# Two more Strassen-like inner products in a layernorm-MLP kernel on Trainium2

## The chip, the cores and the metric

The kernel runs on one core of a Trainium2 chip. The metric is the device time of one execution in microseconds (us), lower is better. Times come from a profiled execution (the profile) and from unprofiled repeats; the median of the runs is what is compared.

## The reference

The kernel computes a layernorm over the last axis, a first matrix product with gelu, and a second matrix product, for 2048 rows, D = 1024 and F = 3584, with bf16 inputs and outputs:

```
def reference(x, w1, b1, w2, b2):
    y = _layernorm(x, axis=-1)
    h = _gelu(jnp.einsum("bsd,df->bsf", y, w1) + b1)
    return jnp.einsum("bsf,fd->bsd", h, w2) + b2
```

## The kernel before

The 2048 rows are worked off in two blocks of 1024 (block 0 and block 1). Each block has a first stage, MM1 (y times w1, with gelu on ScalarE, called ACT), and a second stage, MM2 (h times w2 plus b2). Both use a fast matrix multiplication in place of the plain one: the 2x2 block product is formed from seven products instead of eight, with sums of operand quarters ("S" sums of the left operand, "T" sums of the right one) and sums of the products. The sums run on VectorE (DVE), the matmuls on TensorE (PE).

In MM2 a product, numbered 1 to 7, multiplies a quarter of h, or a sum of quarters (S1 to S4, made in place in h by `sums`, hS1 to hS4), with a quarter of w2 (B11, B12, B21, B22) or a sum of quarters (T1 to T4). T1 to T4 of w2 are made once, in MM1 of block 0, by `w2_prep` (line 702), and stored to a DRAM buffer (`w2_sums`) from which later loads take them. T1 also stays in SBUF, in the slot A of `w2a_sb`; B11 lies in slot B.

A product of MM2 is done in one of two ways:

- plain (`plain`, line 793): four row tiles, 14 matmuls of 512 columns each, 56 in all;
- inner (`inner`, line 838): the same seven-product scheme once more, one level down. Its steps run in the order 1, 5, 6, 2, 7, 3, 4; each is 14 matmuls of 256 columns, 98 in all. It needs four S sums and four T sums of its own (128x1792 elements each, line 681), and copies or additions of PSUM between the steps: step 6 waits for a copy of step 1's result (f1, or s2/k1), step 7 for a copy or an addition of step 6's result (k2), step 4 for an addition after step 7 (r22 or o22). In the form without an output f1, k5, k2, r11 and r21 are ACT copies and r22, r12 DVE additions; in the form with an output k1 and the seed s2 are ACT copies.

Which products are inner is a table, and so is their order:

```
SEQ2 = ((5, 1, 2, 6, 7, 3, 4), (1, 5, 2, 6, 7, 3, 4))
INNER = ((1, 2, 3, 4), (1, 5, 2, 7, 3, 4))
```

So in block 0 products 5, 6 and 7 are plain, and in block 1 product 6 alone. The inner T sums of products 1 to 4 are formed in block 0 by `inner_sums` (line 814) and stored to DRAM (`w_inner_sums`); those of products 5 and 7 are formed in MM1 of block 1 by `t_inner` (line 1130), which loads T1 or T3 back from DRAM. Block 1 loads all of them with `fetch` (line 965), seven loads of 448 KB for a product.

Beside MM2 of block 0 run the x tiles of block 1: `ln_act2` (line 438) does the layernorm of eight tiles on ACT (a sum, a scale, the squares, and at the end the normalization, L459), with three small POOL steps (L450, L453, L456) between the squares and the normalization. Then SP, which issues the DMAs, issues two DMA transposes for each tile (`dma_T`, L488).

The order on every engine is fixed beforehand by a planner (`Planner.place`): each operation has an engine, a cost and a due time, and the planner places it in the engine's queue by these. Each engine then takes its instructions in this order, and waits on semaphores. The buffers that sums are written to are those of MM1 (`t1_sb`, and the three slots of `w1_sb`), as they come free.

Of the kernel before, what the change touches and what calls it, by code (L numbers as in the profile page):

```python
# [23 lines left out]
P = 128  # L24
# [7 lines left out]
SEQ2 = ((5, 1, 2, 6, 7, 3, 4), (1, 5, 2, 6, 7, 3, 4))  # L32
INNER = ((1, 2, 3, 4), (1, 5, 2, 7, 3, 4))
# [203 lines left out]
def bass_standalone__mixer_channel_mlp__prompt_kernel(  # L237
# [24 lines left out]
    with ExitStack() as es:  # L262
# [58 lines left out]
        T_MM2 = TH * 3 * NU * MM512 + 4 * 7 * NU * MM256  # L321
# [112 lines left out]
        junk2 = t1_sb[:, :, :, :, :].rearrange("p a b k c -> p (a b k c)")[:, 7 * D:8 * D]  # L434
# [3 lines left out]
        def ln_act2(s, i, prio, war):  # L438
            war = [*war, *junk_last[-1:]]
            a0 = add("ACT", 1.25, lambda e: e.activation(out=junk2, in_=x_sb[:, i, :], func=ACT.Identity,  # L440
# [4 lines left out]
            a2 = add("ACT", 1.35, lambda e: e.activation(out=junk2, in_=x_sb[:, i, :], func=ACT.Square,  # L445
# [292 lines left out]
        def load_w2(s, slot, what, deps, prio):  # L738
            if what in W2SRC:
                e, c = W2SRC[what]  # L740
                o = dma(w2q[slot], w2v[:, e, :, c * HT:(c + 1) * HT], deps, prio, f"w2_{s}_{what}", f"w2_{slot}",
                        NU * P * HT * 2)
                return w2q[slot], [[o]] * NU
            j = int(what[1]) - 1
            o = dma(w2q16[slot], tq[j], [*deps, *tq_ok[j]], prio, f"w2_{s}_{what}", f"w2_{slot}", NU * P * HT * 2)
            return w2q16[slot], [[o]] * NU
# [3 lines left out]
        def mm2_block(s, W):  # L750
# [3 lines left out]
            for p in SEQ2[s]:  # L754
                pt[p] = t0
                t0 += 7 * SUB if p in inn else TH * SLOT2
            A = {q: (h[q], [[h_ok[(s, q, u)]] for u in range(NU)]) for q in h}
            users = {p: [] for p in SEQ2[s]}
            stores = []
            done = lambda p: users[p]  # L760
# [22 lines left out]
            def dve(fn, deps, at, name, **k):  # L783
                return add("DVE", 0.69, fn, deps, at, name, **k)
# [52 lines left out]

            def inner(p, a, Yo, xb, war, O=None, bias=None, out=None, gate=(), kk=None):

# [60 lines left out]
                hk = Holder(snaps) if kk is None else None  # L900

                def kk_q():
                    t = kk if hk is None else sn_sb[:, hk.k, :]
                    return t.rearrange("p (v c) -> p v c", v=2)
# [5 lines left out]
                k1 = copy(kk_q, lambda: bank_q(c0), (subs[1], *gate), end(1), f"k1_{nm}", alloc=hk)  # L910
                k5 = dve(lambda e: plus(e, quart(g, 1, 1), bank_q(c5), quart(g, 1, 1)), (subs[5], ok[22]), end(5), f"k5_{nm}")
                sub(6, (k1,))
                k2 = dve(lambda e: plus(e, quart(g, 0, 1), bank_q(c0), quart(g, 0, 1)), (subs[6], ok[12]), end(6), f"k2_{nm}")
# [4 lines left out]
                o22 = dve(lambda e: plus(e, o_q(1, 1), bank_q(c0), quart(g, 1, 1)), (subs[7], k5), end(7), f"o22_{nm}",  # L918
                          alloc=ho[1])
                sub(3, (k5,))  # L920
                o12 = dve(lambda e: plus(e, o_q(0, 1), bank_q(c5), quart(g, 0, 1)), (subs[3], k2, o11), end(3), f"o12_{nm}",
                          frees=(c5,))
                if out is not None:
# [3 lines left out]
                          f"o21_{nm}", frees=(c0, g) if out is not None else (c0,))  # L927
                if out is not None:
                    store(out, 2, 2, ho[1], (o22, o21), end(4))
                users[p] += list(subs.values()) + flat(s1, s2, s3, s4)  # L930
                if out is None:
                    return g, {11: o11, 12: o12, 21: o21, 22: o22}, subs
# [6 lines left out]
            X0 = halves(t1_sb[:, :, :, :, :].rearrange("p a b k c -> p (a b k c)"))  # L939
            n = s * NC + NC - 1  # L940
            Y0 = [y for m in (n - 2, n) for y in halves(w1_16[:, m % N_W1].rearrange("p k c -> p (k c)"))[:2]]
            S1 = sums(h[21], A[21], A[22], ALU.add, (), pt[5] - 12, f"hS1_{s}")
            ring = uniq(*(w1_use[m] for m in range(n - 2, n + 1)), *(l for m in (n - 1, n) for l in t1_use[m].values()))
            war0 = {(c, r): ring + S1[1][-1] for c in "ST" for r in range(1, 8)}

            def last_block():
# [39 lines left out]
                def give(names, subs):  # L986
                    for r, b in zip(SEQ1, names):
# [3 lines left out]
                        2: ("W0", "W1", "Y5", "Y6", "Y7", "X0", "X1"), 7: ("B0", "B1", "B2", "B3", "V0", "V1", "Y0"),  # L991
                        3: ("Y1", "Y2", "Y3", "Y4", "W0", "W1", "Y5"), 4: ("Y6", "Y7", "X0", "X1", "A0", "A1", "A2")}
                Yo = {1: fetch(1, hold[1], base1[s] + 0.5 * T_MM1), 5: fetch(5, hold[5], pt[1] - 10),
                      2: fetch(2, hold[2], pt[1])}
                ring_of = lambda m: [*w1_use[m], *(o for l in t1_use[m].values() for o in l)]
                warX = {("S", r): ring_of(n - 1) + (ring_of(n) if r in (7, 3) else []) for r in (5, 6, 7, 3)}
# [10 lines left out]
                B6 = load_w2(s, "A", "T2", [o for k in range(4) for o in use[f"A{k}"]], pt[5])  # L1007
                Yo[7] = fetch(7, hold[7], pt[2])
                hb = [Holder(banks, seeded=True) for _ in range(TH)]
                sdb = seed(1, hb, lambda t: tile_of(g1, t), [(ok1[11], ok1[12]) if t < 2 else (ok1[21], ok1[22])  # L1010
                                                             for t in range(TH)], pt[2])
                S2 = sums(h[11], S1, A[11], ALU.subtract, done(1), pt[5] + 2, f"hS2_{s}", step=(2, 4, 4, 4))
                S3 = sums(h[21], A[22], S2, ALU.subtract, done(5), pt[2] + 4, f"hS3_{s}", step=(4, 4, 4, 2))

                okw = {11: ok1[11], 12: sdb[1], 21: sdb[3], 22: sdb[3]}
                sub2 = inner(2, A[12], Yo[2], XX, war_of(sub1), O=(g1, okw), out=11, gate=W["x"])
# [3 lines left out]

                M6 = plain(6, S2, B6, hb, False, [(o,) for o in sdb])
                g12, gv = Holder(snaps, 4), Holder(snaps, 4)
                O12, V = [], []
                for t in range(TH):
                    at = pt[6] + (t + 1) * SLOT2
                    ok_t = (ok5[11], ok5[12]) if t < 2 else (ok5[21], ok5[22])
                    V.append(copy(lambda t=t: tile_of(gv, t), lambda t=t: bank_t(hb[t]), (M6[t], *V[:1]), at, f"V_{s}_{t}",
                                  alloc=gv if t == 0 else None))
                    O12.append(dve(lambda e, t=t: plus(e, tile_of(g12, t), bank_t(hb[t]), tile_of(g5, t)),
                                   (M6[t], V[t], *ok_t, *O12[:1]), at, f"O12_{s}_{t}", alloc=g12 if t == 0 else None,  # L1030
                                   frees=(hb[t],)))
                for k in range(4):
                    use[f"A{k}"] = list(M6)
                Yo[4] = fetch(4, hold[4], pt[7])

                okv = {11: V[1], 12: V[1], 21: V[3], 22: V[3]}
                gw, okq, sub7 = inner(7, S3, Yo[7], XT, war_of(sub5), O=(gv, okv), kk=dl_sb[:, :], gate=(sub5[5],))
                give(hold[7], sub7)
                for i in range(2):
                    ho = Holder(outs, 2)  # L1040
                    f = []
                    for j in (1, 0):
                        q = 10 * (i + 1) + j + 1
                        f.append(dve(lambda e, i=i, j=j, ho=ho: plus(
                            e, o_sb[:, ho.k:ho.k + 2, j * HI:(j + 1) * HI], quart(gw, i, j), quart(g5, i, j)),
                            (okq[q], O12[3], *f), pt[7] + 7 * SUB + 0.1 * i, f"o22_{s}_{i}{j}",
                            alloc=ho if not f else None, frees=(g5,) if i and not j else ()))
                    store(22, 2 * i, 2, ho, f, pt[7] + 7 * SUB)

                sub3 = inner(3, S4, Yo[3], XX, war_of(sub2),  # L1050
                             O=(g12, {11: O12[1], 12: O12[1], 21: O12[3], 22: O12[3]}), out=12)
                inner(4, A[22], Yo[4], XT, war_of(sub7), O=(gw, okq), out=21,
                      gate=(f[-1],))
# [8 lines left out]
            B = dict(W)  # L1062

            h5 = [Holder(banks, seeded=True) for _ in range(TH)]
            sd5 = seed(5, h5, lambda t: dl_sb[:, :].rearrange("p (j c) -> p j c", j=2), [(bias_ok, jobs[-3])] * 2 + [(bias_ok, jobs[-1])] * 2, pt[5] - 8)
            M5 = plain(5, S1, B[5], h5, False, [(o,) for o in sd5])
            g5 = Holder(snaps, 4)
            O5 = []
            for t in range(TH):
                O5.append(copy(lambda t=t: tile_of(g5, t), lambda t=t: bank_t(h5[t]), (M5[t], *O5[:1]),  # L1070
                               pt[5] + (t + 1) * SLOT2, f"O5_{s}_{t}", alloc=g5 if t == 0 else None, frees=(h5[t],)))

            B[2] = load_w2(s, "C", "B21", W["C"], base2[s])
            B[6] = load_w2(s, "A", "T2", done(5) + tq_ok[0], pt[1])
            hb = [Holder(banks, seeded=True) for _ in range(TH)]
            g1, ok1, sub1 = inner(1, A[11], inner_sums(1, B[1], Y0, war0), X0, war0, gate=(M5[2],), bias=(
# [187 lines left out]
```

## Time and profile before

| | |
|---|---|
| median of 4 runs (range) | 344.26 us (343.61 to 345.03) |
| profiled execution, its time | 345.03 us |
| its span | 343.30 us |
| PE, DVE, ACT, POOL busy | 335.3, 259.3, 184.0, 23.5 us |
| MM1 of block 0 | up to 99.8 us |
| MM2 of block 0: product 5 | 99.80 to 111.88 us |
| MM2 of block 0: products 1, 2, 6, 7, 3, 4 | 111.88 to 184.03 us, overlapping MM1 of block 1 from 174.26 us |
| MM1 of block 1 | to 263.53 us |
| MM2 of block 1 | 263.53 to 339.82 us |

The stages are those of the chain of waits, in which TensorE's groups are merged in order of time. L608 are the matmuls of MM1, L797 those of plain and L864 those of inner products. Instructions of one line in a row are counted with "x", the time from a group's start to the next one's is what the group took on PE. Timelines give start, duration, engine, line, operation, output and inputs; what stands in brackets is the engine's idle time ahead of the instruction and what ended it.

### The profile page before, as it was taken

What the parts mean: (1) busy time and instruction counts of PE and PEld (TensorE: products, weight loads), DVE (VectorE), ACT (ScalarE), POOL (GpSimd) and SP (SyncE); (2) the same over time, 40 slices, a digit from 0 to 9 for tenths busy, and PEclk for the clock granted to TensorE, in tenths of its full rate; (3) what the DMA queues carried; (4) which work ended last, traced back from release to release, by engine and by line L of the source; (5) the groups of instructions that cost most, each with busy time, mean ns of one, the idle gap of its engine ahead of it and who ended that gap; (6) DMA issues with size and microseconds to landing.
All of it is one profiled execution on the core that took longest, in us unless ns stands there. A gap on an engine that the chain in (4) does not pass through costs nothing.

```text
span 343.3 us, 5750 instructions
## 1 busy us (share of the span) xinstructions
PE 335.3 (98%) x2263; PEld 210.5 (61%) x2263; DVE 259.3 (76%) x363; ACT 184.0 (54%) x306; POOL 23.5 (7%) x47
## 2 busy tenths in 40 slices
PE   4999999999999999999999999999999999999995
PEld 4977444444444885547875444444445888658885
DVE  4679988989657599859999559597338968798733
ACT  3774666766788878722113866767676441021110
POOL 2320000000003223320000000000000000000000
PEclk9999999999999999999999999999999999999999
DMA  7748999998969998589798897992133999964111
GB/s 238 254 86 279 351 358 326 298 326 259 352 234 312 292 329 200 110 271 383 255 335 316 264 371 254 338 294 81 68 107 84 352 380 359 344 213 157 63 61 63
DMA packets 75141, 85.98 MB, mean 250 GB/s; under 512 B 13930, under 2 KB 63082, under 8 KB 74346
## 3 DMA queue, kind: packets, MB, share of 16 engines
q1 hardware_dynamic: 74970, 85.48, 76.9%
q8 instruction: 18, 0.29, 0.3%
q10 hardware_dynamic: 144, 0.13, 0.2%
q14 instruction: 9, 0.07, 0.1%
HBM read 60.43 MB, written 22.54 MB: 242 GB/s over the span
## 4 chain that ended last, share of the span: by engine, by line
PE 97%; DMA 1%; ACT 1%; SPq 0%; DVE 0%; issue 0%
PE ps L608 46%; PE ps L864 31%; PE ps L797 14%; PE ps L566 5%; DMA x_sb<-in_x_dram 1%; PE ps L472 1%; ACT h_sb L414 0%; SPq L327 0%; DVE o_sb L761 0%; ACT yw_sb L479 0%; ACT mv_sb L416 0%; PE ps L383 0%
## 5 line engine op out<-in xcount | busy, mean ns | idle before, releaser
L608 PE MATMUL ps<-yw_sb,t_sb 128*128 128x512 f16 x416 | 96.2, 379 | 0.0
L608 PE MATMUL ps<-yw_sb,w_sb 128*128 128x512 f16 x312 | 73.7, 379 | 0.0
L608 PEld LDWEIGHTS ps<-yw_sb,t_sb 128*128 128x128 f16 x416 | 40.6, 98 | 48.8 <-ACT ps L621 0.4
L608 PEld LDWEIGHTS ps<-yw_sb,w_sb 128*128 128x128 bf16 x312 | 30.4, 98 | 36.2 <-ACT ps L621 0.3
L626 DVE TENSOR_TENSOR sn_sb<-ps,sn_sb 128x512 f32<-128x512 f32 x54 | 36.2, 687 | 18.2 <-PE ps L608 17.9
L797 PE MATMUL ps<-w2a_sb,h_sb 128*128 128x512 f16 x224 | 49.3, 379 | 0.0
L632 ACT ACTIVATE h_sb<-sn_sb,b_sb 128x512 f16<-128x512 f32 x54 | 38.1, 718 | 19.8 <-DVE sn_sb L626 17.9
L681 DVE TENSOR_TENSOR h_sb<-h_sb 128x1024 f16<-128x1024 f16 (+2 forms) x42 | 38.6, 952 | 2.9 <-ACT h_sb L632 2.1
L632 ACT ACTIVATE h_sb<-ps,b_sb 128x512 f16<-128x512 f32 x50 | 34.1, 683 | 10.5 <-PE ps L608 9.3
L621 ACT COPY sn_sb<-ps 128x512 f32<-128x512 f32 x50 | 29.1, 587 | 18.9 <-PE ps L608 18.7
L797 PEld LDWEIGHTS ps<-w2a_sb,h_sb 128*128 128x128 f16 x224 | 21.9, 98 | 25.4
L781 ACT COPY sn_sb<-ps 128x512 f32<-128x512 f32 x30 | 17.3, 581 | 33.0 <-PE ps L797 19.4
L761 DVE TENSOR_TENSOR o_sb<-ps,sn_sb 128x512 bf16<-128x512 f32 x28 | 19.1, 689 | 13.4 <-PE ps L864 11.9
L761 DVE TENSOR_TENSOR sn_sb<-ps,sn_sb 128x512 f32<-128x512 f32 x31 | 21.3, 687 | 9.7 <-PE ps L864 8.9
L781 ACT COPY ps<-sn_sb 128x512 f32<-128x512 f32 x15 | 8.8, 589 | 34.3 <-PE ps L864 30.4
L864 PE MATMUL ps<-w2a_sb,h_sb 128*128 128x256 f16 (+1 forms) x196 | 23.5, 273 | 0.0
L864 PE MATMUL ps<-w_sb,t_sb 128*128 128x256 f16 x182 | 21.7, 273 | 0.0
L864 PEld LDWEIGHTS ps<-w2a_sb,h_sb 128*128 128x128 f16 x196 | 19.2, 98 | 3.3
L541 DVE TENSOR_TENSOR t_sb<-w_sb,t_sb 128x1024 f16<-128x1024 bf16 x26 | 17.9, 688 | 3.2 <-PE ps L608 2.5
L864 PEld LDWEIGHTS ps<-w_sb,t_sb 128*128 128x128 f16 x182 | 17.8, 98 | 2.3
L541 DVE TENSOR_TENSOR t_sb<-w_sb 128x1024 f16<-128x1024 bf16 x26 | 17.7, 682 | 0.2 <-PE ps L608 0.2
L566 PE MATMUL ps<-yw_sb,w_sb 128*128 128x128 f16 x256 | 16.6, 228 | 0.9 <-ACT yw_sb L479 0.9
(91 smaller groups left out, 374.2 us busy)
## 6 DMA issues: line engine op xcount, KB each, us to landing
w_sb<-in_w_dram SPq DMA_DIRECT2D x28, 512.0 KB, 6.4
x_sb<-in_w_dram SPq DMA_DIRECT2D x21, 256.0 KB, 5.1
w_sums<-x_sb SPq DMA_DIRECT2D x21, 256.0 KB, 5.0
w_inner_sums<-w_sb SPq DMA_DIRECT2D x12, 448.0 KB, 5.3
w2a_sb<-w_sums SPq DMA_DIRECT2D x3, 1792.0 KB, 8.6
yw_sb<-w_inner_sums SPq DMA_DIRECT2D x10, 448.0 KB, 8.0
x_sb<-in_x_dram SPq DMA_DIRECT2D x15, 256.0 KB, 6.3
w2a_sb<-in_w_dram SPq DMA_DIRECT2D x2, 1792.0 KB, 9.5
```

Of the source, the lines that this page charges most:

```text
L472: fn = [(lambda e, j=j, k=k, hold=hold: e.transpose(out=ps16[:, hold.k, j * P:(j + 1) * P], in_=x16[:, i, k * HT + j * P:k * HT + (j + 1) ...
L541: return add("DVE", 0.65, lambda e: e.tensor_tensor(out=tv(k), in0=x0, in1=x1, op=ALU.subtract), [*deps, *war.get(k, ())], prio + 0.5 * k, ...
L566: fn = [(lambda e, b=b, hb=hold[f], f=f, k=k, t=t: e.matmul(ps[:, hb.k, t * P:(t + 1) * P], lhsT=lhs[:, k, f * P:(f + 1) * P], rhs=yop[f"A ...
L608: fn = [(lambda e, k=k: e.matmul(ps[:, hold[p].k, :], lhsT=lhs[:, k, :], rhs=yop[yo][:, k, :], start=(first and k == 0), stop=(k == KH - 1 ...
L621: return e.copy(out=dst, in_=src) if o_.eng == "ACT" else e.tensor_copy(dst, src)
L626: return add("DVE", 0.69, lambda e: e.tensor_tensor(out=sn_sb[:, hold_s.k, :], in0=ps[:, hold[p].k, :], in1=sn_sb[:, hold_s.k, :], op=ALU. ...
L632: r = h_ok[(s, q, u)] = add("ACT", 0.70, lambda e: e.activation(out=h[q][:, u, :], in_=src(), func=ACT.Gelu_apprx_tanh, bias=b1_sb[:, f:f ...
L681: o = add("DVE", cost2(w * dst.shape[-1]), lambda e, k0=k0, k1=k1: e.tensor_tensor(out=dst[:, k0:k1, :], in0=a[0][:, k0:k1, :], in1=b[0][: ...
L761: plus = lambda e, out, x, y: e.tensor_tensor(out=out, in0=x, in1=y, op=ALU.add)
L781: return act(lambda e: e.copy(out=out(), in_=src()), deps, at, name, **k)
L797: fn = [(lambda e, k=k, t=t: e.matmul(ps[:, banks_[t].k, :], lhsT=a[0][:, k, t * P:(t + 1) * P], rhs=b[0][:, k, :], start=(first and k == ...
L864: fn = [(lambda e, k=k, j=j: e.matmul(ps[:, bank[r].k, j * HI:(j + 1) * HI], lhsT=x[0][:, k, j * P:(j + 1) * P], rhs=y[0][:, k, :], start= ...
```

## The change

Product 5 of block 0 and product 6 of block 1 become inner products, so that five are inner in block 0 and all seven in block 1; both blocks open with product 1. The T sums of T1 (product 5) are formed in block 0 from the T1 that lies in slot A, and `t_inner` makes those of T2 (product 6) in their place. Buffers move with this: the T sums of product 1 go to the w1 slots of the last two chunks, those of product 5 to the slot of the third-last chunk and to the output buffer `o_sb`; the scratch output of the layernorm passes moves to the tails of `t1_sb`. T2's load into slot A is split in two halves. In block 1 `inner` gets a form with a separate target (`tmp`), and the sums of product results O12 and o22 become two additions of double width each. The due times of the DVE additions in MM2 are 2.5 us earlier.

```
-SEQ2 = ((5, 1, 2, 6, 7, 3, 4), (1, 5, 2, 6, 7, 3, 4))
-INNER = ((1, 2, 3, 4), (1, 5, 2, 7, 3, 4))
+SEQ2 = (1, 5, 2, 6, 7, 3, 4)
+INNER = ((1, 5, 2, 3, 4), SEQ2)
...
-        T_MM2 = TH * 3 * NU * MM512 + 4 * 7 * NU * MM256
+        T_MM2 = TH * (7 - len(INNER[0])) * NU * MM512 + len(INNER[0]) * 7 * NU * MM256
...
             def dve(fn, deps, at, name, **k):
-                return add("DVE", 0.69, fn, deps, at, name, **k)
+                return add("DVE", 0.69, fn, deps, at - 2.5, name, **k)
...
-                B6 = load_w2(s, "A", "T2", [o for k in range(4) for o in use[f"A{k}"]], pt[5])
+                Yo[6] = fetch(6, hold[6], pt[5])
...
-                M6 = plain(6, S2, B6, hb, False, [(o,) for o in sdb])
...
+                _, okv, sub6 = inner(6, S2, Yo[6], XT, war_of(sub5), O=(g1, {q: last_[q] for q in ok1}))
...
-            h5 = [Holder(banks, seeded=True) for _ in range(TH)]
-            sd5 = seed(5, h5, lambda t: dl_sb[:, :].rearrange("p (j c) -> p j c", j=2), [(bias_ok, jobs[-3])] * 2 + [(bias_ok, jobs[-1])] * 2, pt[5] - 8)
-            M5 = plain(5, S1, B[5], h5, False, [(o,) for o in sd5])
...
-            B[6] = load_w2(s, "A", "T2", done(5) + tq_ok[0], pt[1])
+
+            war1 = warX | {("T", r): w1_use[n if r in (7, 4) else n - 1] for r in (5, 6, 7, 4)}
+            g1, ok1, sub1 = inner(1, A[11], inner_sums(1, B[1], Y0, war1), X0, war1, gate=(jobs[-3],), bias=(
+                b2_sb[:, None, 0:HI].to_broadcast([P, 2, HI]), e0_sb[:, None, :].to_broadcast([P, 2, HI])))
+
+            o_16 = o_sb[:, :, :].bitcast(FP16).rearrange("p n c -> p (n c)")
+            Y5 = halves(w1_16[:, (n - 2) % N_W1].rearrange("p k c -> p (k c)"))[:2] + halves(o_16)[:2]
+            g5, ok5, sub5 = inner(5, S1, inner_sums(5, B[5], Y5, {("T", r): w1_use[n - 2] for r in (5, 6)}), X0,
+                                  war_of(sub1), gate=(sub1[6],), bias=(
+                dl_sb[:, None, 0:HI].to_broadcast([P, 2, HI]), e1_sb[:, None, :].to_broadcast([P, 2, HI])))
+            B[6] = load_w2(s, "A", "T2", done(5) + tq_ok[0], pt[1], 2)
...
-                e5 = t_inner(5, 0, x_end, base1[s] + 0.15 * T_MM1)
-                e7 = t_inner(7, 2, e5, base1[s] + 0.4 * T_MM1)
+                e6 = t_inner(6, 1, x_end, base1[s] + 0.2 * T_MM1)
+                e7 = t_inner(7, 2, e6, base1[s] + 0.45 * T_MM1)
```

## The prediction

> **What bounds the kernel now.** I read the page's busy table first, then the chain of waits, then the engine timelines around block 0 (99.8 to 184 us), where the change works.
>
> ```profile
> PE 335.3 (98%) x2263; PEld 210.5 (61%) x2263; DVE 259.3 (76%) x363; ACT 184.0 (54%) x306; POOL 23.5 (7%) x47
> PE 97%; DMA 1%; ACT 1%; SPq 0%; DVE 0%; issue 0%
> ```
>
> The second line is the chain by engine: TensorE (PE) carries 97% of the span. The list of PE's waits has 4.5 us, all before the first weight product. So from 8.5 to 339.8 us the time is the number of matmuls times their spacing, and any new wait of PE adds in full. The merged chain gives both spacings:
>
> ```profile
> 99.80 12.09 PE ps L797 x56
> ...
> 307.71 32.11 PE ps L864 x294
> ```
>
> A plain product is 56 matmuls of 512 columns, 12.09 us (216 ns each); an inner product is 98 of 256 columns, 32.11/3 = 10.70 us (109 ns each). One product changed over is worth 1.39 us of PE.
>
> In block 0 the engine that feeds PE is ACT: it copies PSUM out between steps and normalizes block 1's eight x tiles, each with a trip to POOL, and it takes its instructions in order. From ACT's and POOL's timelines:
>
> ```profile
> 110.67 1.15 ACT L445 ACTIVATE t_sb<-x_sb,mv_sb 128x1024 f16<-128x1024 bf16 x1
> ...
> 113.97 1.24 ACT L459 ACTIVATE x_sb<-x_sb,st_sb,rstd_sb 128x1024 f16<-128x1024 bf16 x1
> ...
> 143.54 1.24 ACT L459 ACTIVATE x_sb<-x_sb,st_sb,rstd_sb 128x1024 f16<-128x1024 bf16 x1 [2.20 <-POOL st_sb L456]
> ```
> ```profile
> 112.27 0.55 POOL L453 TENSOR_TENSOR rstd_sb<-vpe_sb,nhalf 128x1 f32<-128x1 f32 x1
> 112.90 0.19 POOL L456 TENSOR_TENSOR st_sb<-mv_sb,rstd_sb 128x1 f32<-128x1 f32 x1
> ...
> 141.32 1.41 POOL L453 TENSOR_TENSOR rstd_sb<-vpe_sb,nhalf 128x1 f32<-128x1 f32 x1
> 142.81 0.70 POOL L456 TENSOR_TENSOR st_sb<-mv_sb,rstd_sb 128x1 f32<-128x1 f32 x1
> ```
>
> The reader is to see ACT standing still for 2.20 us ahead of L459 because POOL was slow. From the end of the squares' readout to the end of L456 the eight trips took 2.84, 1.18, 1.55, 2.57, 2.38, 1.17, 3.41 and 2.78 us (mean 2.24). I call this p.
>
> **What the Trainium skill says.** "TensorE: Matmul & The Clock Gate", section "Back-to-back issue gap", gives N/2.4 + 2.5 ns for an isolated matmul: 109 and 216 ns, which the trace shows in the stream too. "SBUF — State Buffer", section "Who interferes with whom", says that a VectorE (DVE) instruction with two SBUF inputs contends with a GpSimd (POOL) instruction that reads SBUF. The trace fits: the 0.55 us trip step at 112.27 fell where DVE was idle, the 1.41 us one at 141.32 inside DVE's sums. "DMA: Bandwidth & Descriptors" ("Anatomy of one DMA") says that semaphore waits are held on the issuing sequencer; in SP's timeline the load of B22 stands behind transposes that wait for ACT.
>
> **The change part by part**, with the order of the changed program's instructions beside the old one. Block 0 opens at 99.80; I keep the old clock and write d for PE's delay.
>
> 1. Product 5 of block 0 and product 6 of block 1 become inner: 2 x (12.09 - 10.70) = **-2.78 us**. Both lie wholly on the chain. PE's list shows it: 112 wide matmuls fewer, 196 narrow ones more.
>
> 2. MM1 of block 0. The old program could spend the 12.09 us of product 5 on product 1's inner sums (L681, 1.00 us apart on DVE). Now product 1 opens, so two of its T sums, two S sums and three T sums of product 5 move ahead of 99.8. DVE was busy 7.29 us of 80 to 90 and 5.94 of 90 to 99.8: 6.6 us free, and the gaps at 87 and 93.5 (1.90 and 2.17 us) take four of them. S5 of product 1 waits for the last gelu of h11 (95.34) and pushes the two L626 sums from 95.52 to 96.4; PE's last product needs them at 98.1. Cost 0, about 0.8 us of room. If that cover failed, each further 1.0 us sum would show whole.
>
> 3. The inner sums of T1 leave block 1 (t_inner takes T2 instead: same four sums and four stores), so block 0 gains four stores of 448 KB, 4 x 1.1 us of the queue. DVE gains 8 sums and 2 additions, 9.2 us, against 14.3 us idle between 99.8 and 184 (69.94 busy of 84.2). No sum comes later than its PE step by my count. The four stores of product 1's sums, which S2's sums wait for, land near 110.1, before product 1 ends at 110.5. Cost 0. ACT loses four seeds and four copies and gains seven copies: about even.
>
> 4. **ACT's order in product 5.** PE's steps, each 1.528 us: 5.1 at 110.50, 5.5, 5.6, 5.2, 5.3, then 5.7 at 118.14, 2.1 at 119.66, 5.4 at 121.19, 2.5, 2.6 at 124.25. Step 5.7 needs k2 of step 5.6, and on ACT k2 now stands behind the normalization (L459) of x tile 1. ACT's spacing is 0.49 (copy), 0.61 (gelu), 1.05 (sum), 0.23 (scale), 1.25 (squares), 1.14 (L459). From the end of step 1.1: f1 101.99, last gelu 102.60, sum 103.65, copies and two bias seeds to 106.57, squares 0 by 108.0, L459 of tile 0 at 108.0 + p = 110.4, r21 112.05, f1 of product 5 (after step 5.1) 112.68, squares 1 at 114.16. Then k2 is ready at 114.16 + p + 1.14 + 0.59 + 0.1, a wait of p - 2.16. I take p = 2.5, above the mean since DVE is full of sums there: **+0.4** (0 to 1.2).
>
> 5. Step 2.6 needs k1 of product 2, behind tile 2's L459: squares 2 end at 120.35, L459 122.85 to 123.99, r21 124.48, k1 ready 125.1, against 124.65: **+0.5** (0 to 1.2).
>
> 6. T2 is loaded into slot A in two halves only when product 5 ends, at 123.1. Whole loads of 1792 KB took 8.1 and 8.6 us (T2, T3 before), so the second half lands at 131.2 to 131.7; the eighth matmul of product 6 wants it at 128.83 + 0.9 + 1.5 = 131.2. **+0.3** (0 to 0.7).
>
> 7. Product 3's load of B22 is issued by SP after the transpose of tile 6. Tile 2's L459 starts at 122.85; squares 3 end at 127.5; each later tile takes 1.14 + 0.23 + 1.25 + p = 5.0 us (p = 2.4, the mean of tiles 3 to 6 before), so tile 6 is normalized at 146.0, and the load issued at 147.3 after a 1.2 us transpose:
>
> ```profile
> 147.42 0.58 SPq L327 DMA_DIRECT2D w2a_sb<-in_w_dram  x1
> ```
> ```profile
> 154.97 1.09 DVE L681 TENSOR_TENSOR w_sb<-w2a_sb 128x1792 f16<-128x1792 bf16 x1 [2.83 <-DMA w2a_sb<-in_w_dram]
> ```
>    In the old run it took 7.55 us. ACT's order also puts O3 of the last tile before the seed of step 3.2, so this seed ends 5.4 us after the landing: 160.25, against PE's 160.52 - 1.39 + 1.2 = 160.33. **0** as counted, with almost no room: each 0.1 us on p adds 0.4 here, once it binds, in place of the waits above.
>
> 8. Block 1. Product 6's operands come as seven loads (3.1 MB for 1.8), DVE gains four S sums and six additions (7.6 us) against 19 us idle after 263.5, and loses eight additions to four of double width. No row shows a 128x1024 f32 addition; the 512-wide from SBUF took 0.69, and "VectorE: DVE Perf Modes" ("The perf-mode tier table") has 2.29 us for 2048 elements, so between 0.69 and 2.3; I take 1.2, and it is not on the path. Four seeds and four V copies go. DMA share is 0.15 after 318 us, so 1.35 MB (about 3.4 us of queue) has room. Reordered DVE dues (2.5 us earlier) cost or gain nothing that I can show: +-0.3. **0**.
>
> Sum: -2.78 + 0.4 + 0.5 + 0.3 = **-1.6 us**. The profiled execution took 345.03 us for a span of 343.30 (1.73 around it), so it would take 343.4; the median of the runs is 344.26, 0.77 lower, so I forecast **342.7**.
>
> **The rivals.**
> - *No new wait* (p near 1.2 when it matters, as at tiles 1 and 5, and loads at 7.5 us): all of -2.78, 341.5. For it: old block 0 had as many such joins and no PE wait. Chance 0.27.
> - *As counted*, p about 2 to 2.5: -2.3 to -0.9, 342.0 to 343.4. Chance 0.37.
> - *ACT's tile chain becomes the bound*: one late normalization after another delays the B22 load, and PE stands before steps 3.1 and 3.2. With p = 2.8 for all tiles tile 6 ends 2.2 us later, the load lands at 157.05, step 3.2 starts at 162.45: 1.9 us late, total +0.5 (344.8). With p = 3.1 it is about +2.3 (346.6), slower. It is slower by over 0.3% once the load lands after 157.5, that is p above 2.9. For it: five of eight trips took 2.3 us or more, and DVE gets fuller. Against: their mean is 2.24. Chance 0.36 from partly to wholly, 0.15 of it slower.
> - *The change doesn't do what it says*: excluded by PE's list.
>
> **How the numbers follow.** 0.3% is 1.03 us, about what a measurement of this kernel can tell from no change. Faster by more: the first rival, nearly all of the second and a few of the third, 0.62. Within: 0.23. Slower: 0.15. The range runs from 341.4 (no new wait, with 0.1 of scatter) to 344.8 (the third at p = 2.8).
>
> **What would show it.** PE's wait list with `ps` steps waiting for ACT `sn_sb` near 118 and 124 and for the seed near 160 shows 4, 5 and 7; a wait on DMA `w2a_sb<-w_sums` near 131 shows 6. No PE wait at all would make the first rival right; a B22 issue after 149 the third. The whole is wrong if block 1 takes any wait, or if PE's matmul spacing leaves 109 and 216 ns.

## The result and the profile after

The kernel before took 344.77 us (median of 56 runs), the changed kernel 344.68 us (35 runs). The ratio is 0.9996, 95% interval 0.9985 to 1.0008: no difference that can be measured. The forecast was 342.7 us. Two of the 35 runs took over 350 us; such slow runs come with other kernels of this document too (349.98 in e10), and the ratios leave them out.

The profiled execution after took 344.84 us for a span of 343.1 (before: 345.03 and 343.30). First the page's busy line of TensorE (PE) and the chain by engine:

```profile
PE 333.2 (97%) x2347; PEld 218.6 (64%) x2347; DVE 275.7 (80%) x379; ACT 180.5 (53%) x299; POOL 21.1 (6%) x47
PE 92%; DMA 3%; POOL 1%; ACT 1%; DVE 1%; issue 1%; SPq 0%
```

PE has 84 matmuls more (112 wide ones fewer, 196 narrow ones more) and 2.1 us less of busy time. But PE's share of the chain fell from 97% to 92%, and a DMA, POOL and ACT now stand in it. The list of PE's waits of the kernel after says which (engine, line, what was waited for: us in total, times, longest):

```profile
PE ps L805 <- DMA w2a_sb<-w_sums: 1.5, 2, 1.0
...
PE ps L873 <- ACT sn_sb L789: 0.7, 1, 0.7
```

L805 is the plain matmul, L873 the inner one. The merged chain of the kernel after gives the places (start, length, what):

```profile
99.62 12.24 PE ps L873 x112
...
114.67 1.42 POOL rstd_sb L453
...
118.03 0.57 ACT sn_sb L789
...
118.65 4.77 PE ps L873 x42
...
123.55 0.32 SPq L327
123.91 8.75 DMA w2a_sb<-w_sums
...
132.71 4.71 PE ps L805 x21
...
183.46 81.26 PE ps L608 x376
264.72 74.90 PE ps L873 x686
```

The reader is to see two breaks in PE's row, both in block 0: one before step 5.7 at 118.65, behind POOL and ACT, and one inside product 6, behind the load of T2. Block 1's 686 inner matmuls then run without a break. PE's timeline sizes the second break, and SP's timeline shows what was issued ahead of T2:

```profile
127.83 1.69 PE L873 MATMUL ps<-w_sb,t_sb 128*128 128x256 f16 x14
130.49 1.68 PE L805 MATMUL ps<-w2a_sb,h_sb 128*128 128x512 f16 x7 [0.97 <-DMA w2a_sb<-w_sums]
132.71 4.71 PE L805 MATMUL ps<-w2a_sb,h_sb 128*128 128x512 f16 x21 [0.54 <-DMA w2a_sb<-w_sums]
```
```profile
119.39 0.58 SPq L327 DMA_DIRECT2D w_inner_sums<-w_sb  x1
120.02 1.36 SPq L488 DMA_TRANSPOSE yw_sb<-x_sb  x1
121.42 1.24 SPq L327 DMA_DIRECT2D w_inner_sums<-w_sb  x1
123.55 0.82 SPq L327 DMA_DIRECT2D w2a_sb<-w_sums  x2
```

Product 6's first 28 matmuls took from 129.52 (127.83 + 1.69) to 137.42, 7.90 us; 28 x 0.216 is 6.04. So T2 cost 1.85 us: the two idle times in brackets, 0.97 and 0.54, and about 0.17 after each until the matmuls follow each other at their spacing again, which is called the refill here. Both halves were late: they landed at 130.44 and 132.66. Step 5.7 started 2.38 us after step 5.3 (116.27) instead of 1.53, so it cost 0.87 with the refill. One more 0.11 us is in block 1's first matmul. From the start of block 0's first weight product in PE's timeline to the start of the last DVE addition, the stretch that the change works on, it is 240.21 us before (99.63 to 339.84) and 240.19 after (99.45 to 339.64), a difference of -0.02. The account is -2.78 + 0.87 + 1.85 + 0.11 = +0.05. The profile closes: **the matmul saving of 2.78 us is all there, and 2.72 us of waits in block 0 take nearly all of it back.**

### The profile page after: what moved, and what is told of

The parts are those of the page before. It is cut to its first block, busy times and chain, and to the rows that moved or that the text cites. A ratio compares the mean times of both kernels' runs of the same rounds, so it can differ in the third digit from the quotient of the medians.

```text
span 343.1 us, 5959 instructions
## 1 busy us (share of the span) xinstructions
PE 333.2 (97%) x2347; PEld 218.6 (64%) x2347; DVE 275.7 (80%) x379; ACT 180.5 (53%) x299; POOL 21.1 (6%) x47
## 4 chain that ended last, share of the span: by engine, by line
PE 92%; DMA 3%; POOL 1%; ACT 1%; DVE 1%; issue 1%; SPq 0%
PE ps L608 46%; PE ps L873 34%; PE ps L805 7%; PE ps L566 5%; DMA w2a_sb<-w_sums 3%; PE ps L472 1%; DMA x_sb<-in_x_dram 1%; POOL rstd_sb L453 0%; DVE st_sb L395 0%; ACT t_sb L445 0%; POOL st_sb L456 0%; DVE o_sb L769 0%; POOL vpe_sb L450 0%; ACT yw_sb L479 0%; ACT sn_sb L789 0%
## 5 line engine op out<-in xcount | busy, mean ns | idle before, releaser
L626 DVE TENSOR_TENSOR sn_sb<-ps,sn_sb 128x512 f32<-128x512 f32 x54 | 36.0, 687 | 13.7 <-PE ps L608 13.5
L621 ACT COPY sn_sb<-ps 128x512 f32<-128x512 f32 x51 | 29.9, 586 | 20.6 <-PE ps L608 20.3
L873 PE MATMUL ps<-w2a_sb,h_sb 128*128 128x256 f16 (+1 forms) x266 | 32.1, 273 | 0.0
L769 DVE TENSOR_TENSOR sn_sb<-ps,sn_sb 128x512 f32<-128x512 f32 x35 | 24.0, 687 | 9.3 <-PE ps L873 5.5
L789 ACT COPY sn_sb<-ps 128x512 f32<-128x512 f32 x27 | 15.5, 581 | 28.9 <-DVE o_sb L769 16.4
L873 PEld LDWEIGHTS ps<-w2a_sb,h_sb 128*128 128x128 f16 x266 | 26.0, 98 | 4.1
L805 PE MATMUL ps<-w2a_sb,h_sb 128*128 128x512 f16 x112 | 24.7, 379 | 1.5 <-DMA w2a_sb<-w_sums 1.5
L873 PE MATMUL ps<-w_sb,t_sb 128*128 128x256 f16 x196 | 23.2, 273 | 0.0
L541 DVE TENSOR_TENSOR t_sb<-w_sb 128x1024 f16<-128x1024 bf16 x26 | 17.7, 682 | 5.8 <-DMA w_sb<-in_w_dram 4.4
L789 ACT COPY ps<-sn_sb 128x512 f32<-128x512 f32 x12 | 7.0, 585 | 27.5 <-PE ps L873 26.6
L873 PEld LDWEIGHTS ps<-w_sb,t_sb 128*128 128x128 f16 x196 | 19.2, 98 | 2.2
L541 DVE TENSOR_TENSOR t_sb<-w_sb,t_sb 128x1024 f16<-128x1024 bf16 x26 | 17.9, 688 | 3.3 <-PE ps L608 2.1
L805 PEld LDWEIGHTS ps<-w2a_sb,h_sb 128*128 128x128 f16 x112 | 10.8, 98 | 14.8 <-DMA w2a_sb<-w_sums 2.3
```

The source lines that it names most:

```text
L541: return add("DVE", 0.65, lambda e: e.tensor_tensor(out=tv(k), in0=x0, in1=x1, op=ALU.subtract), [*deps, *war.get(k, ())], prio + 0.5 * k, ...
L621: return e.copy(out=dst, in_=src) if o_.eng == "ACT" else e.tensor_copy(dst, src)
L626: return add("DVE", 0.69, lambda e: e.tensor_tensor(out=sn_sb[:, hold_s.k, :], in0=ps[:, hold[p].k, :], in1=sn_sb[:, hold_s.k, :], op=ALU. ...
L769: plus = lambda e, out, x, y: e.tensor_tensor(out=out, in0=x, in1=y, op=ALU.add)
L789: return act(lambda e: e.copy(out=out(), in_=src()), deps, at, name, **k)
L805: fn = [(lambda e, k=k, t=t: e.matmul(ps[:, banks_[t].k, :], lhsT=a[0][:, k, t * P:(t + 1) * P], rhs=b[0][:, k, :], start=(first and k == ...
```

## The experiments

What comes before that stretch (loads and the first tiles) moves by up to 2.6 us between profiled executions whatever the kernel: the first weight product started between 98.36 and 100.94. So profiles are compared below by the stretch, the timed runs by their ratio to runs of the kernel before that were taken with them. e1 to e4 ran on one chip, e5 to e8 on a second, e9 to e12 on a third; e4 and e12, the same kernel on two of them, gave 0.9936 and 0.9937. "Stretch" is its change against the kernel before's 240.21 us.

The theory (A): each inner product saves its 1.39 us; block 1 keeps it; block 0 loses 2.7 us to two waits, for T2 and for k2. Rivals are named in the expectations.

| run | stretch, us | wait at 5.7 | wait in product 6 | block 1's first matmul | median, us | ratio to before (95%) |
|---|---|---|---|---|---|---|
| changed kernel | -0.02 | 0.87 | 1.85 | 0.11 | 344.68 | 0.9996 (0.9985 to 1.0008) |
| e1 block 1 only | -1.43 | no such step | 0 | 0 | 343.53 | 0.9969 (0.9956 to 0.9983) |
| e6 block 0 only | +2.81 | 0.55 | 1.64 | 0.43 | 346.11 | 1.0043 (1.0027 to 1.0059) |
| e2 T2 in slot B | -1.89 | 0.95 | 0 | 0 | 342.39 | 0.9935 (0.9910 to 0.9959) |
| e3 k2 first | -0.39 | 0 | 1.58 | 0.64 | 344.73 | 1.0002 (0.9983 to 1.0020) |
| e4 both | -2.66 | 0 | 0 | 0 | 342.53 | 0.9936 (0.9916 to 0.9956) |
| e5 T2 ahead of stores | -1.10 | 0.74 | 0.17 | 0.85 | 344.83 | 1.0002 (0.9986 to 1.0017) |
| e7 T2 whole | +0.76 | 1.38 | 2.23 | 0 | 345.86 | 1.0041 (1.0019 to 1.0062) |
| e8 slots and ACT order | -2.01 | 0 | 0 | 0 | 342.53 | 0.9935 (0.9915 to 0.9955) |
| e9 w1 sums later | -0.66 | 0.67 | 1.52 | 0 | 343.62 | 0.9957 (0.9939 to 0.9976) |
| e10 = e5 + e9 | -1.61 | 0.67 | 0.28 | 0.16 | 344.09 | 0.9965 (0.9947 to 0.9983) |
| e11 = e3 + e9 | -0.73 | 0 | 2.12 | 0 | 343.67 | 0.9967 (0.9952 to 0.9983) |
| e12 = e4 again | -2.51 | 0 | 0 | 0 | 342.33 | 0.9937 (0.9915 to 0.9959) |

The waits are worked out from the ends of PE's groups against 1.53 us for an inner step, 3.02 for a plain tile and 0.86 for a four-matmul group of the first stage; those under 0.1 are shown as 0, and waits at other steps, which e3, e4, e6, e8 and e12 have, stand outside the table. One profile is no finer than some tenths: e9 and the changed kernel are the same in block 0, and their waits there are 0.67 and 1.52 against 0.87 and 1.85.

### The two halves of the change: e1 and e6

e1 takes block 1 of the changed kernel and block 0 of the kernel before.

```
-SEQ2 = (1, 5, 2, 6, 7, 3, 4)
-INNER = ((1, 5, 2, 3, 4), SEQ2)
+SEQ2 = ((5, 1, 2, 6, 7, 3, 4), (1, 5, 2, 6, 7, 3, 4))
+INNER = ((1, 2, 3, 4), SEQ2[1])
...
+                e5 = t_inner(5, 0, x_end, base1[s] + 0.1 * T_MM1)
```

> Block 0 as in the kernel before (product 5 plain, five-first order), block 1 as in the changed kernel (all seven products inner); the sums of T1, T2 and T3 are then all formed during block 1's first matmul. Theory A (each inner product saves 1.39 us of TensorE; block 1 keeps its 1.39, block 0 loses its own 1.39 to two new waits): 1.39 us under the kernel before, ratio 0.996, no new TensorE wait. Rival B (product 6's seven small loads or the added VectorE sums give time back in block 1 as well, and the change is worth nothing anywhere): ratio 1.000.

e6 is the other half.

```
-INNER = ((1, 5, 2, 3, 4), SEQ2)
+INNER = ((1, 5, 2, 3, 4), (1, 5, 2, 7, 3, 4))
```

> Block 0 as in the changed kernel (product 1 first, product 5 inner), block 1 as in the kernel before (product 6 plain). Theory A: -1.39 us of TensorE work, +0.87 of wait at step 5.7, +1.85 at product 6: 1.3 us slower than the kernel before, ratio 1.004. Rival E (the two blocks share the loss, e.g. through block 1's extra loads and sums): ratio 1.000 or below.

e1's merged chain ends in one piece from block 1's first inner matmul on, as in the changed kernel:

```profile
264.79 74.90 PE ps L873 x686
```

Before, those products took 339.82 - 263.53 = 76.29 us, so block 1 saves 1.39; the stretch is 1.43 shorter and the median 1.03. Rival B falls. Block 0 alone is slower by 0.43% (1.5 us; theory 1.3). **One half of the change was a gain and the other a loss of about the same size.** That rival E falls with this is not shown: the loss comes with block 0's half of the edit, but part of it sits in block 1's first matmul.

e6's profile has more waits than the changed kernel's. The largest is 1.6 us at step 5.4, which the prediction counted at nothing. Its DVE timeline shows where it came from:

```profile
109.31 1.10 DVE L681 TENSOR_TENSOR t_sb<-h_sb,t_sb 128x1792 f16<-128x1792 f16 x1
113.45 1.83 DVE L681 TENSOR_TENSOR h_sb<-h_sb 128x1024 f16<-128x1024 f16 x2 [3.05 <-DMA w_inner_sums<-w_sb]
```

DVE stood 3.05 us in front of S2's sums until a store of product 1's T sums had landed; all behind it came later, r22 of step 5.7 too, for which step 5.4 waits. In the changed kernel's profile the same wait was 1.10 us and PE did not feel it. The last of those stores landed at 113.23 here and at 111.48 there.

e6 also has the order of VectorE in block 1's first matmul that is the subject of e9 below:

```profile
201.69 0.69 DVE L541 TENSOR_TENSOR t_sb<-w_sb 128x1024 f16<-128x1024 bf16 x1 [5.02 <-DMA w_sb<-in_w_dram]
202.30 0.68 DVE L626 TENSOR_TENSOR sn_sb<-ps,sn_sb 128x512 f32<-128x512 f32 x1
```

It cost 0.43 us in this profile. If it costs the timed runs of e6 what it costs those of three other kernels below (an estimate: no run took it out of e6), about 1.3 of the 1.5 us are due to it, and the agreement with theory A's 1.3 is chance.

### T2's landing: e2, e5, e7

e2 exchanges the slots of T2 and T3 (B22 and the T sums of product 4 follow).

```
-            B[6] = load_w2(s, "A", "T2", done(5) + tq_ok[0], pt[1], 2)
...
-            B[7] = load_w2(s, "B", "T3", done(1), pt[5])
+            B[6] = load_w2(s, "B", "T2", done(1), pt[5])
+            B[7] = load_w2(s, "A", "T3", done(5) + tq_ok[0], pt[1])
```

> The changed kernel with the slots of T2 and T3 exchanged: T2 goes to slot B, which product 1 leaves at 110.4, in one load, and T3 to slot A, which product 5 leaves at about 123. Product 6 then finds T2 some 10 us early, T3 has until about 140. Theory A (product 6 loses 1.85 us to T2's landing): the PE wait of L805 on DMA w2a_sb<-w_sums goes, 1.85 us under the changed kernel, ratio 0.995 to the kernel before. Rival B (the tile chain on ACT and the load of B22 behind tile 6's transposes set when product 3 can begin, so a PE that comes earlier waits there): at most 0.5 us under the changed kernel, with a PE wait at step 3.1 or 3.5 on w2a_sb or w_sb.

Its merged chain has product 6 behind product 2 without a break, 6.04 us for 28 matmuls, and no wait at step 3.1 or 3.5:

```profile
118.11 10.87 PE ps L873 x98
128.99 6.04 PE ps L805 x28
```

The stretch is 1.87 us shorter than the changed kernel's, with k2's wait still there: in the profile theory A, to the size, and rival B falls. The timed runs fall 0.0061 x 344.7 = 2.1 us. Not all of that need be T2: the planner changed DVE's order in block 1's first matmul here as well (e9 below).

e5 leaves the slots and moves T2's two loads ahead of two stores in SP's order.

```
         order = pl.place()
+        q = order["SP"]
+        for name in ("w2_0_T2_0", "w2_0_T2_1"):
+            o = next(o for o in q if o.name == name)
+            q.remove(o)
+            q.insert([p.name for p in q].index("is2_1"), o)
```

(`is2_1` is the store of product 2's first T sum.)

> The changed kernel with the two half loads of T2 issued by SP ahead of the stores of product 2's first two sums (they stood right behind them); these stores then wait on SP until product 5 has ended, and nothing else is moved. Theory A2 (T2 lands late because 0.9 MB of stores issued just before it take the DMA engines first, not because slot A comes free late): the halves land near 127.5 and 130 instead of 130.4 and 132.7, product 6 waits 0 to 0.3 us instead of 1.85, 1.6 us under the changed kernel, ratio 0.996. Rival D (product 5's end alone is too late for T2, 6.1 us before its first use): the landing moves by less than 0.5 us and the time stays at 1.000.

e5's SP timeline has T2 first and the stores behind it. The transpose that stood between the stores is now behind T2 too, so the edit moves three transfers and not two:

```profile
122.41 0.80 SPq L327 DMA_DIRECT2D w2a_sb<-w_sums  x2
123.26 0.43 SPq L327 DMA_DIRECT2D w_inner_sums<-w_sb  x1
123.73 1.48 SPq L488 DMA_TRANSPOSE yw_sb<-x_sb  x1
125.25 1.13 SPq L327 DMA_DIRECT2D w_inner_sums<-w_sb  x2
```

The halves landed at 127.25 and 129.85, that is 28.6 and 31.2 us after the end of the first stage's matmuls, against 30.8 and 33.0 in the changed kernel. The wait in product 6 went from 1.85 to 0.17. In the profile A2 holds and D falls: T2 was late because of what was issued just before it, 0.9 MB of stores and a transpose; these were not tested apart. e10 below has the same order of SP and the same landing (28.6 and 31.3 us). This fits what the Trainium skill's "DMA: Bandwidth & Descriptors", section "Queues, rings and completion order", says, that on each DMA engine descriptors are consumed in ring order. The timed runs did not follow: 1.0002. So the place of the loads in the queue is shown to set the wait of the profiled executions (0.17 us here, 0.28 in e10), not to bring the time down.

e7 takes the split into halves away.

```
-            B[6] = load_w2(s, "A", "T2", done(5) + tq_ok[0], pt[1], 2)
+            B[6] = load_w2(s, "A", "T2", done(5) + tq_ok[0], pt[1], 1)
```

> The changed kernel with T2 loaded as one transfer instead of two halves (1792 KB after product 5's end). Theory A: product 6 has to wait for the whole of it, which lands near 132.7, against a first use at 129.5: 3.1 us of wait instead of 1.85, 1.3 us slower than the changed kernel, ratio 1.0036. Rival F (the two halves get in each other's way and one transfer lands by 131.1, as the 7.5 us of other whole loads say): 1.55 us of wait, 0.3 us faster than the changed kernel.

e7's PE timeline:

```profile
131.00 3.19 PE L805 MATMUL ps<-w2a_sb,h_sb 128*128 128x512 f16 x14 [2.06 <-DMA w2a_sb<-w_sums]
```

With the refill the wait is 2.23 us instead of 1.85, between the two expectations; the median is 1.2 us above the changed kernel's, as theory A had it, and the intervals of the two ratios do not meet. But the planner also changed DVE's order in block 1's first matmul here, which is worth about 1.3 us (e9 below), and on PE 14 matmuls of product 6 instead of 28 now stand ahead of steps 2.3 and 2.4. Against e9, which has the first two of these additions ahead too, e7 is 0.0084 x 344.7 = 2.9 us slower (1.4 in the stretch). So the agreement with A's figure is chance: by these runs the split is worth more than A said, and no trace shows why. In the profile the whole load landed 8.1 us after product 5's end, between the two halves of the changed kernel (7.0 and 9.2).

### ACT's order: e3, e4, e8

```
         order = pl.place()
+        act = order["ACT"]
+        names = [o.name for o in act]
+        act.insert(names.index("y1_1"), act.pop(names.index("k2_5_0")))
```

(`k2_5_0` is k2 of product 5 in block 0, `y1_1` the L459 of tile 1.)

> The changed kernel with one ACT instruction moved: the copy k2 of product 5 stands ahead of the normalization (L459) of x tile 1. Theory A: step 5.7 no longer waits 0.87 us, product 5 ends 0.87 earlier, T2's load is issued 0.87 earlier and lands as much earlier: 0.87 us under the changed kernel, ratio 0.997 or 0.998 to the kernel before. Rival C (T2's landing is set by the traffic ahead of it in the queue and not by product 5's end): the wait of product 6 grows from 1.85 to 2.7 us and the time stays as in the changed kernel, ratio 1.000.

The wait at step 5.7 is gone from e3's profile. Counted from the end of the first stage's matmuls, product 5 ended after 22.94 us instead of 23.81, T2's halves landed after 29.95 and 32.14 instead of 30.82 and 33.04, and product 6 ended 0.9 us earlier. Up to there the profile has theory A's gain, though the scatter of T2's landing is half as large (e9, with the changed kernel's block 0, has 32.52). T2's issue moved by 0.2 us alone. e3's merged chain:

```profile
113.61 8.70 DMA w_inner_sums<-o_sb
...
122.37 0.32 SPq L327
...
122.73 8.03 DMA w2a_sb<-w_sums
...
130.80 4.71 PE ps L805 x21
```

T2's load waits for product 5's matmuls and for the stores of its T sums. With the matmuls earlier (product 5 ended at 121.55), a store that took 8.70 us from issue to landing released the load at 122.3, 0.8 us after PE; the load then took 8.4 us from the first half's issue to the second half's landing, against 9.1. Step 2.6 lost 0.24 us and block 1's first matmul 0.64 (next part), and the timed runs stayed at 1.0002. That is the ratio of rival C without its mechanism: product 6's wait did not grow to 2.7 but was 1.58. e4 has the edits of e2 and e3 together.

> Both edits at once: T2 in slot B, T3 in slot A, and k2 of product 5 ahead of tile 1's normalization. Theory A: both waits go, 2.7 us under the changed kernel and the kernel before, ratio 0.992, near 342.0 us. Rival B (the B22 load is next): 1 to 1.5 us less than that, ratio 0.996, with PE waiting at step 3.1 or 3.5.

e4's merged chain runs through all of it; the one place left is step 2.6 at 123.98, which with the refill took 0.19 us too long:

```profile
99.52 24.45 PE ps L873 x224
...
123.98 4.76 PE ps L873 x42
128.74 6.04 PE ps L805 x28
```

The stretch is 2.66 us shorter than before, of the 2.78 of the account, and the ratio is 0.9936. Rival B falls. e8 adds two more such moves, for step 2.6:

```
+        for name, first in (("k2_5_0", "y1_1"), ("r21_5_0", "y1_2"), ("k1_2_0", "y1_2")):
+            names = [o.name for o in act]
+            o = act.pop(names.index(name))
+            act.insert(names.index(first), o)
```

> The changed kernel with T2 in slot B and T3 in slot A, k2 of product 5 ahead of tile 1's normalization, and the copies r21 of product 5 and k1 of product 2 ahead of tile 2's. Theory A: besides the two large waits the 0.2 us at step 2.6 that appeared in their place goes as well; 2.8 us under the kernel before, ratio 0.992, no TensorE wait after the first matmul. Rival B (tile 2's normalization 1 us later delays the tile chain and the load of B22, so that PE waits at step 3.1 or 3.5): 0.5 to 1 us less than that, 0.994 to 0.995.

The 0.2 us at step 2.6 went, and 0.43 at step 2.3, 0.17 at 5.4 and 0.25 at 3.7 came. No gain (0.9935): with each wait removed there, another one of some tenths appears. So A's "no wait" did not come, and neither did B's wait at step 3.1 or 3.5.

### What the changed kernel's profile hardly shows: e9 to e12

e3 and e5 both took a wait away in block 0 and got nothing. Both had a new one in block 1's first matmul. e5's DVE timeline:

```profile
197.60 0.69 DVE L541 TENSOR_TENSOR t_sb<-w_sb 128x1024 f16<-128x1024 bf16 x1 [4.56 <-DMA w_sb<-in_w_dram]
198.21 0.68 DVE L626 TENSOR_TENSOR sn_sb<-ps,sn_sb 128x512 f32<-128x512 f32 x1
199.82 0.69 DVE L541 TENSOR_TENSOR t_sb<-w_sb,t_sb 128x1024 f16<-128x1024 bf16 x1 [0.93 <-DMA w_sb<-in_w_dram]
200.43 1.88 DVE L626 TENSOR_TENSOR sn_sb<-ps,sn_sb 128x512 f32<-128x512 f32 x3
```

Two sums of w1 (L541) stand on DVE ahead of the L626 additions that PE waits for, and they wait for a load of w1. In the kernel before they stand behind; its L626 additions wait for PE alone:

```profile
198.74 0.69 DVE L626 TENSOR_TENSOR sn_sb<-ps,sn_sb 128x512 f32<-128x512 f32 x1 [4.75 <-PE ps L608]
199.61 0.69 DVE L626 TENSOR_TENSOR sn_sb<-ps,sn_sb 128x512 f32<-128x512 f32 x1 [0.17 <-PE ps L608]
...
207.66 0.68 DVE L541 TENSOR_TENSOR t_sb<-w_sb 128x1024 f16<-128x1024 bf16 x1
```

The changed kernel has e5's order, and there the second half of the load landed at 201.88, with the addition behind it 0.1 us late for PE. e9 moves the two sums (`w1T1_1_3`, `w1T2_1_3`) behind the second of those additions (`c7_1_3`), in the changed kernel, and nothing else.

```
+        q = order["DVE"]
+        at = next(o for o in q if o.name == "c7_1_3")
+        late = [o for o in q if o.name in ('w1T1_1_3', 'w1T2_1_3')]
+        q[:] = [o for o in q if o not in late]
+        k = q.index(at) + 1
+        q[k:k] = late
```

> The changed kernel with two VectorE instructions moved: the sums of w1's fourth column group (L541, they wait for a load that lands at about 200) stand behind the two L626 additions of the pair of units before, instead of ahead of them. Theory G (in the timed runs this load is often later than in the profiled one, VectorE then holds up the L626 additions and PE waits in block 1's first matmul; that is why the run without T2's wait, e5, shows no gain in its timed runs and why the changed kernel's slowest runs reach 351): the median falls 0.5 to 1.5 us under the changed kernel, ratio 0.996 to 0.998, and the slowest runs come down. Rival H (the spread comes from T2's landing in block 0 alone): no change, ratio 1.000.

e9's DVE timeline has the L626 additions first, waiting for PE alone:

```profile
199.17 0.69 DVE L626 TENSOR_TENSOR sn_sb<-ps,sn_sb 128x512 f32<-128x512 f32 x1 [4.29 <-PE ps L608]
200.03 0.69 DVE L626 TENSOR_TENSOR sn_sb<-ps,sn_sb 128x512 f32<-128x512 f32 x1 [0.17 <-PE ps L608]
200.64 0.68 DVE L541 TENSOR_TENSOR t_sb<-w_sb 128x1024 f16<-128x1024 bf16 x1
```

The ratio went from 0.9996 to 0.9957, and the two intervals do not meet: 0.0039 of 344.7, about 1.3 us, within G's 0.5 to 1.5, though the ratio lies just under its 0.996. The same edit did the same on e5 (e10, which is e5's and e9's edits, 1.0002 to 0.9965) and on e3 (e11, e3's and e9's edits, 1.0002 to 0.9967), 1.2 to 1.3 us each. So H falls, and the place of these two sums is shown to cost the timed runs over a microsecond. G's reason for it, a load of w1 that is later in the timed runs than in the profiled one, is argued and not shown, since the timed runs have no trace. In the profiles of these three the order had cost 0.11, 0.85 and 0.64 us. (The stretch of e9 is 0.64 us shorter than the changed kernel's; 0.53 of this lies in block 0, which the edit leaves alone.)

> Both: T2's halves ahead of the stores in the queue and the sums of w1's fourth column group behind the L626 additions. Theory G: the profile loses both waits, T2's (1.85) and the one that took its place in block 1's first matmul (0.85), and the timed runs fall with it: 1.9 us under the kernel before, ratio 0.9945, near 342.8. Rival I (T2 is late again in the timed runs, since where it stands in the queue doesn't settle its landing): 0.5 us or less under the kernel before.

e10's profile has both waits small, as G said, but its time does not lie below e9's (0.9965 against 0.9957), and the 0.9945 that G gave is just outside the interval. T2 ahead of the stores is worth nothing that can be measured in the timed runs, with either order of DVE. Rival I would say why, though its number (0.5 us or less under the kernel before) failed too, as e9's edit alone brings 1.5; the timed runs have no trace, so it stays open.

> The sums of w1's fourth column group behind the L626 additions, as in e9, and k2 of product 5 ahead of tile 1's normalization, as in e3. With e9, e2 and e4 this closes a square (k2 late or first, T2 late or early) in which VectorE's order in block 1's first matmul is the same. Theory A: step 5.7's 0.7 to 0.9 us of wait goes and T2's issue comes with it; 0.5 to 0.9 us under e9, ratio 0.993 to 0.9945 to the kernel before, with T2's wait (about 1.5) still in the profile. Rival C (with product 5 ending earlier, the store of its last sum holds T2's load, as in e3's profile, and product 6 waits longer): 0.3 us or less under e9, ratio 0.995 to 0.996.

No gain over e9 again: here rival C, in the profile too. In e11's merged chain T2's second half took 9.02 us:

```profile
122.56 9.02 DMA w2a_sb<-w_sums
```

Counted from the end of the first stage's matmuls, the load was issued when product 5 ended, 0.66 us earlier than in e9 (23.07 for 23.73), but its second half landed only 0.07 earlier (32.45 for 32.52), and product 6 waited 2.12 us instead of 1.52. What k2 gave, T2 took in this profile; in e3's it did not. Three pairs differ by k2's place alone: e3 and the changed kernel, e11 and e9, e4 and e2. In none did k2 first bring the ratio down (it rose by 0.0006, 0.0010 and 0.0001), so the 0.7 to 0.95 us at step 5.7 are seen in profiles only (the intervals would hide some of it).

> The kernel of e4 once more, on the same chip as e11, from which it differs by T2 in slot B and T3 in slot A and what the planner makes of it. Theory A (T2's landing costs 1.5 to 1.85 us in the timed runs as in the profile): 1.5 us under e11, ratio 0.992 to 0.9935. Rival J (the timed runs lose little on T2, and e2's and e4's gain over the changed kernel was VectorE's order in block 1): within 0.5 us of e11.

The kernel of e4 again, at 0.9937, and 1.3 us (of the medians) under e11 on the same chip: the exchange of slots does save time in the timed runs. By the ratios it is 0.8 us (e9 to e2) and 1.0 us (e11 to e12), less than the profile's 1.5 to 2.1, but these intervals overlap, so the size isn't settled. Rival J's 0.5 us is too little by the medians and not excluded by the intervals.

That all of it is T2's landing isn't shown either, since the expectation of e11 is not quite right: VectorE's order is not the same. In e9, e10 and e11 the two sums of w1 still stand ahead of the next L626 additions and wait for their load, as e10's DVE timeline shows; in e2, e4 and e12 they stand behind these as well (e12: L541 at 205.66).

```profile
201.69 0.69 DVE L541 TENSOR_TENSOR t_sb<-w_sb,t_sb 128x1024 f16<-128x1024 bf16 x1 [1.06 <-DMA w_sb<-in_w_dram]
202.30 1.28 DVE L626 TENSOR_TENSOR sn_sb<-ps,sn_sb 128x512 f32<-128x512 f32 x2
```

In e10's profile this cost PE 0.16 us. e7 has the sums behind all four additions too, with T2 whole in slot A, and is 3.7 us (0.0106) slower than e2: which points to T2's landing as a cost in the timed runs, at least when it is loaded whole. For the two halves, no run has this order with T2 in slot A, and how much of the gain is T2's and how much the order's stays open.

**e2, e4, e8 and e12, the runs with T2 in slot B, beat both kernels**, by 0.6% (interval 0.4% to 0.9%), some 2.2 us. Between them the runs do not tell.

## Why the prediction was wrong, step by step

The forecast of 342.7 was too low by what three waits took in the profile, of which the timed runs show two (T2's and DVE's). Its likeliest case and 0.62 of its chance stood on a gain that did not come. That its range held the result is luck: 344.8 was the end of the third rival, the late load of B22, which did not come either.

1. *-2.78 us.* Right: e1's and e4's stretches are 1.43 and 2.66 us shorter, and the spacing stayed at 109 and 216 ns.
2. *Product 1's sums hidden in the first stage.* Right: steps 1.1 to 1.4 ran without a wait.
3. *Block 0's extra stores and sums at 0.* PE took no wait from them in the changed kernel's profile, but the landing was wrong: product 1's stores landed at 111.48, not 110.1, after product 1's end at 110.33, so DVE stood 1.10 us before S2. In e6's profile the same store came 2.0 us later, counted from the end of the first stage (13.8 and 11.85 us after it), and cost PE 1.6 us. The cover was thinner than the step said.
4. *k2 behind tile 1's normalization.* Right mechanism, term too small: p was 3.01 us for this tile, not 2.5 (squares read out by 113.85, L456 ended at 116.86), so 0.87 us and not 0.4; inside the 0 to 1.2 given. POOL's 1.41 us instruction lay inside DVE's sums, as the prediction read the old trace.
5. *Step 2.6 behind tile 2's.* 0 instead of 0.5: this trip took 1.67 us (120.47 to 122.14). Where step 5.7 no longer waited, it showed (0.24 in e3, 0.19 in e4).
6. *T2's two halves.* **The step that failed in the profile:** 1.85 us, not 0.3 and outside its range of 0 to 0.7. It took a whole load's 8.1 to 8.6 us from product 5's end; the second half landed 9.2 us after it (132.66 against 123.43). And it tested only the second half: the first was due at 129.5, 6.1 us after product 5's end, and landed after 7.0, which is the larger part of the wait (0.97 and its refill). Two stores of product 2's sums, issued at 119.39 and 121.42, and a transpose between them stood ahead of it, which the step did not list; e5 shows that they made the difference in the profile.
7. *B22.* Right: the load was issued at 146.55 and landed at 153.75, PE took no wait for it in the changed kernel, and the third rival did not come.
8. *Block 1 at 0, +-0.3.* Right for the products (74.90 us in one piece, no wait); the additions of double width took 1.22 us, as the step took them (1.2). **Wrong for the block's first matmul**, which the step did not look at beyond "reordered DVE dues". w1's fourth column group is now loaded ahead of t_inner's first load instead of behind it and lands earlier (200.15 for 203.67), and its sums now stand ahead of L626 on DVE, which stands still for them. In e1, e2, e4, e7, e8 and e12, where t_inner's load stands ahead again, so do the L626 additions. Why the planner turns the two is not shown: t_inner's load is due later than before (0.2 for 0.15 of the first stage), but in e2, e4, e7, e8 and e12 it is due at 0.2 too. The prediction had called itself wrong if block 1 takes any wait, and this is that wait. It is 0.11 us in the profile and, by e9, e10 and e11, about 1.3 us in the timed runs.

In the timed runs, +1.3 us is measured for DVE's order and +0.8 to 1.0 for T2 in slot A. With the -2.78, which is measured in the profiles only, 0.4 to 0.6 us are left to reach the measured -0.1; this is within the intervals. The best kernels, without these waits, are 2.2 us under the kernel before and not 2.78.

What stays open: why T2 ahead of the stores, and k2 ahead of the normalization, shorten the profiled execution and not the timed ones, why DVE's order costs the timed runs more than the profiled ones, and how much of the gain from the exchanged slots is T2's landing. That POOL's trip sets p was read from the traces; no run took POOL out of it.

## What to carry to other kernels

When a product is made faster, what is loaded when it ends is due earlier: cost such a load with the transfers that stand ahead of it in the queue, and test every part of it against its own first use. Prefer a buffer that comes free early over a better place in the queue: exchanging two slots (with what it moved on DVE) brought 0.8 to 1.0 us in the timed runs where moving the load brought nothing. And look through the whole order of each engine for an instruction that waits for a load and has moved ahead of one that the bottleneck needs; a tenth of a microsecond of wait in one profile may be a microsecond in the runs.

## What was not expected of the hardware

- A store of 448 KB took 8.70 us from issue to landing in e3, among the transfers of block 0; T2's 1792 KB in two halves landed 9.2 us after product 5's end in the changed kernel and 7.6 us after it with two stores and a transpose out of the way (e5: 129.85, product 5 ended at 122.29).
- One normalization trip over POOL took 3.01 us and the next 1.67 in the same profile.
